# Attention in a planned kernel: the steps of all head pairs placed by a table of times, and squares in halves on ScalarE

## The chip, the core and the metric

One core of one Trainium2 chip runs the whole program. The metric is the device time of one execution in microseconds, taken as the median of the runs. The kernel before took 1324.17 us (three runs, 1322.8 to 1329.11 us).

## What is computed

Attention over 4 batches, 12 heads, 448 tokens and a head size of 64, with RMS-normed q and k, and then two dense MLPs over 1792 tokens, all in 32-bit floats.

```
q_n, k_n = rmsnorm(q, g_q), rmsnorm(k, g_k)      # x / sqrt(mean(x*x) + 1e-6) * g, over the head size
scores = (1/sqrt(64)) * q_n @ k_n.T ; scores -= max(scores) ; attn = exp(scores)
attn = attn / (sum(attn) + 1e-9) ; out = attn @ v                      # q, k, v: (4, 12, 448, 64)
x = out as (1792, 768)
h = x @ w_in ; x = (h * sigmoid(h)) @ w_out                            # w_in (768, 2048), w_out (2048, 768)
h = x @ w_in2 ; y = relu(h)**2 @ w_out2
```

## The kernel before

The program makes a list of **steps** and a planner orders them. `Plan.step` records a step with its engine or engines and an assumed duration; buffers come from rings of fixed depth (`RINGS` for SBUF, `BANKS` for PSUM: 4 banks `s`, 3 banks `t`, 1 bank `pv`). `Plan.forward` is a list scheduler: at each turn it takes, over all engines, the ready step that can start first, and among equals the one that is due first. `Plan.backward` makes new due times from the result, six rounds in all, and `Plan.issue` writes the instructions in the order of the best round. Each engine then executes its own instructions strictly in that order, and waits on semaphores. Buffers of a ring are handed on in the order in which the source creates them (`Buf.turn`), whatever the planner does.

Attention works on 24 **pairs** of heads (4 batches x 6). For a pair:

- `prepare` (L442): q and k are loaded by SP (L452, ring `qk` of 3), squared into `sq` (L461 on ScalarE for the first three pairs, L463 on GpSimd for the rest; one instruction of 1024 elements for q and k together), summed on VectorE (L474), turned into inverse roots by three Newton rounds of small GpSimd instructions (L481, L499 to L511) with two small VectorE ones (L487, L493), and multiplied in (`norm`, L519: GpSimd, for the first pairs also VectorE). TensorE transposes the normed q and k (L530), and ScalarE and VectorE split the result into a high part (L540, L538) and a low part (L547, L545).
- `weigh` (L566): for each of 4 chunks of 112 rows: six matmuls make the scores of two heads in two `s` banks (L579), VectorE takes the row maxima (L589), ScalarE the exponentials and their sums (L595), TensorE transposes them into `t` banks (L603), and ScalarE (L417) or VectorE (L419) copies them to `PT`. `ECOPY` (L35) allows ScalarE for the first head's copy, either engine for the second's.
- `attend` (L613): the sums are inverted (L621, L622), stored to DRAM as 896 numbers of 4 bytes (L628, `store_r`, by SP or ScalarE's queue) and read back broadcast into `R` (L636, `spread`); TensorE multiplies `PT` by v into the bank `pv` (L647); ScalarE copies it out and VectorE or GpSimd multiplies by `R` (L668, `attended`).

The result `xf` of the first two batches is split into the MLP's operand (`x_hi`, `x_lo`, the helper's lines L429, L431 and L438); that of the last two is stored (L699) and read back later. The first MLP (L862 up, L916 down) and the second (L1081, L1157) follow on TensorE. Their weights arrive as 64-bit words that are squeezed into floats on ScalarE (L761) and VectorE (L765 to L781), and split in two parts (L429, L431, L438); a few of these units are made during attention and fill gaps there. The new pool of buffers behind attention opens when all attention steps have been issued, and its first tiles wait for the last store of `xf`.

A step's engines and its assumed time are written like this, here `squares`:

```
"squares", at, {**act_t(2 * W2), **pool_t(2 * W2, 600.0)} if i < SOON else pool_t(2 * W2, 600.0), squares,
reads=[(qk, 0), (qk, 1)], writes=[sq],
```

Of the kernel before, what the change touches and what calls it, by code (L numbers as in the profile page):

```python
# [24 lines left out]
RINGS = {"xb": 4, "yb": 2, "yf": 5, "xl": 2, "v": 1, "V": 2, "part": 2, "xf": 6, "raw": 2, "W": 3, "w": 5, "E": 4, "PT": 4, "qk": 3, "T": 2, "n": 2, "vv": 3, "g": 4}  # L25
# [7 lines left out]
SOON = 3  # L33

ECOPY = [[("act",), ("act", "dve")]] * 4  # L35
# [15 lines left out]
class Step:  # L51
    def __init__(self, kind, on, fn, when, n):
        self.kind, self.on, self.fn, self.when, self.n = kind, on, fn, when, n
        self.needs, self.claims = {}, []
        self.at = min(on, key=lambda e: on[e][0])
        self.extra = 4.5 if kind == "store_r" else 0.0

# [9 lines left out]
class Plan:  # L67
# [42 lines left out]

    def link(self):

        pre = [dict() for _ in self.steps]
# [19 lines left out]
    def forward(self, due):  # L133
# [12 lines left out]
        span = 0.0  # L146
        while len(order) < len(steps):
            best = None
            for e in ENGINES:
                f = free[e]  # L150
                for n in wait[e]:
# [19 lines left out]
            if best is None:  # L171
                raise RuntimeError("no step can be issued")
            (st, _, _), e, n = best
            s = steps[n]
            t, xfer, locks = s.on[e]
            if xfer is not None:
# [120 lines left out]
def kernel(  # L297
# [144 lines left out]
    def prepare(i):  # L442
# [6 lines left out]
        for n, src in enumerate((q, k)):  # L449
# [6 lines left out]
            )  # L456
        sq = sa([CP, 2, NB8, D], F32, "sq", 1)

        def squares(e):
            if e == "act":  # L460
                nc.scalar.activation(sq.ap, qk.ap, AF.Square)  # L461
            else:
                engine(e).tensor_tensor(sq.ap, qk.ap, qk.ap, ALU.mult)  # L463

        step(
            "squares", at, {**act_t(2 * W2), **pool_t(2 * W2, 600.0)} if i < SOON else pool_t(2 * W2, 600.0), squares,
            reads=[(qk, 0), (qk, 1)], writes=[sq],
        )
# [6 lines left out]
            reads=[sq], writes=[ms],  # L475
        )

        little = {"pool": (0.17, None, True)}
# [4 lines left out]
        )  # L483

# [5 lines left out]
        )  # L490
        step(
# [5 lines left out]
        for _ in range(3):  # L497
# [3 lines left out]
            )  # L501
            step(
                "newton", at, little, lambda e: nc.gpsimd.tensor_tensor(a.ap, a.ap, ms.ap, ALU.mult),
                reads=[ms], writes=[a],
            )
            step(
                "newton", at, little,
                lambda e: nc.gpsimd.tensor_scalar(a.ap, a.ap, 1.5, None, ALU.add), writes=[a],
            )
            step(  # L510
                "newton", at, little, lambda e: nc.gpsimd.tensor_tensor(y.ap, a.ap, y.ap, ALU.mult),  # L511
                reads=[a], writes=[y],
            )
        T = sa([P, 2, 2, S], FR, "T")
        for n in range(2):
            n32 = sa([CP, NCH, 2, D], F32, "n")
            step(
                "norm", at, any_t(W2, 600.0) if i < SOON else pool_t(W2, 600.0),
# [6 lines left out]
            )  # L525
            pt = psum("t")
# [726 lines left out]
```

## Time and profile before

| | |
|---|---|
| median of 3 runs | 1324.17 us |
| the profiled execution | 1326.16 us, of which its span is 1324.4 us |
| mean granted TensorE clock | 0.977 |
| TensorE busy | 1219.7 us (92%) |
| VectorE busy | 939.1 us (71%) |
| ScalarE busy | 530.8 us (40%) |
| GpSimd busy | 250.8 us (19%) |

The page and the trace come from one execution. Attention takes roughly the first 400 us of it, the first MLP the time to about 860 us, the second the rest. "PE" is TensorE's matmuls, "PEld" its weight loads, which overlap them; DVE is VectorE, ACT is ScalarE, POOL is GpSimd, SP the engine that issues most DMAs. A busy share over the whole span mixes these three stages; the stage that a change touches has to be read by itself. An arrow in a row names what ended the idle time before the instruction.

### The profile page before, as it was taken

Reading aid. Unit: us, or ns where it says so; the run is one execution under the profiler, and the core shown is the slowest. Engines: PE = TensorE matmul, PEld = TensorE weight load, DVE = VectorE, ACT = ScalarE, POOL = GpSimd, SP = SyncE. Lnnn points to the kernel's source line nnn. Section 1 sums busy time; section 2 is a strip of 40 time slices with the busy share of each in tenths; the row PEclk is TensorE's granted clock in tenths of the full one; section 3 lists DMA queues with packets and bytes.
Section 4 is the critical chain, followed back from the end, with each engine's and each line's share of the span. In section 5 each row is a group of like instructions: output and inputs, shape, how many; then the busy total and the mean of one; then the engine's idle time right before and its main releaser. Section 6 shows DMA issues by size and latency. Waiting matters only on the chain. (4 is left out here: it accounts for less than half of the span.)

```text
span 1324.4 us, 18981 instructions
## 1 busy us (share of the span) xinstructions
PE 1219.7 (92%) x6960; PEld 1069.2 (81%) x6960; DVE 939.1 (71%) x1618; ACT 530.8 (40%) x1117; POOL 250.8 (19%) x443
## 2 busy tenths in 40 slices
PE   5678788788899999999999998999999998999998
PEld 3455555556679999989999997989988998999998
DVE  6677766566658798778889887866677885445554
ACT  4666665566644332243433322343333333122111
POOL 5666545445200000010100000101121100000000
PEclk9889988889999999999999999999999999999999
DMA  5465433444325555549687784784456767445434
GB/s 144 87 119 109 104 81 57 76 87 77 51 39 181 156 161 156 151 138 334 215 261 243 224 258 149 239 319 179 179 186 228 279 244 237 172 148 181 155 132 131
DMA packets 134109, 220.75 MB, mean 167 GB/s; under 512 B 31104, under 2 KB 99456, under 8 KB 134016
## 3 DMA queue, kind: packets, MB, share of 16 engines
q1 hardware_dynamic: 119264, 219.25, 54.6%
q10 hardware_dynamic: 14752, 0.29, 0.6%
q8 instruction: 55, 0.90, 0.3%
q14 instruction: 38, 0.31, 0.1%
HBM read 145.88 MB, written 73.62 MB: 166 GB/s over the span
## 5 line engine op out<-in xcount | busy, mean ns | idle before, releaser
L862 PE MATMUL t<-xb,w 128*128 128x448 f32 x1152 | 242.5, 367 | 5.1 <-DVE g L879 4.9
L916 PE MATMUL s<-gg,w 128*128 128x448 f32 x1152 | 240.6, 366 | 1.3 <-DVE gg L438 1.3
L862 PEld LDWEIGHTS t<-xb,w 128*128 128x128 f32 x1152 | 217.3, 189 | 24.1 <-DVE g L879 6.0
L916 PEld LDWEIGHTS s<-gg,w 128*128 128x128 f32 x1152 | 216.2, 188 | 19.4 <-DVE gg L438 1.7
L1157 PE MATMUL s<-w,gh 128*128 128x384 f32 x896 | 228.0, 335 | 0.0
L1157 PEld LDWEIGHTS s<-w,gh 128*128 128x128 f32 x896 | 162.5, 188 | 1.9 <-DVE gg L1184 0.3
L1157 PE MATMUL s<-w,gl 128*128 128x384 f32 x448 | 150.5, 336 | 6.0 <-DVE gl L438 5.9
L1184 DVE TENSOR_TENSOR gg<-s,gg 128x384 f32<-128x384 f32 x196 | 107.5, 554 | 55.0 <-PE s L1157 54.8
L589 DVE TENSOR_REDUCE mx<-s 112x1 f32<-112x448 f32 x192 | 108.6, 617 | 52.4 <-PE s L579 37.1
L603 PEld LDWEIGHTS t<-ident,E 112*112 112x112 f32 x768 | 78.0, 140 | 74.4 <-ACT E L595 42.8
L603 PE MATMUL t<-ident,E 112*112 112x112 f32 x768 | 105.2, 278 | 34.0 <-ACT E L595 28.5
L595 ACT ACTIVATE E<-s,mx 112x448 f32<-112x448 f32 x192 | 121.5, 654 | 25.8 <-DVE mx L589 25.8
L438 POOL TENSOR_TENSOR w<-W,w 128x768 fp32r<-128x768 f32 (+1 forms) x18 | 30.9, 1719 | 487.4 <-ACT w L429 483.5
L1097 DVE TENSOR_TENSOR g<-t,g 128x448 f32<-128x448 f32 x96 | 58.2, 620 | 85.3 <-ACT g L417 57.4
L647 PE MATMUL pv<-PT,vv 112*64 112x224 f32 x768 | 94.8, 382 | 0.2 <-DVE PT L419 0.2
L579 PE MATMUL s<-T 64*112 64x448 f32 x576 | 88.3, 420 | 5.4 <-DVE T L545 4.6
L417 ACT COPY PT<-t 112x448 f32<-112x448 f32 x133 | 69.7, 556 | 56.9 <-PE t L530 21.3
L1157 PEld LDWEIGHTS s<-w,gl 128*128 128x128 f32 x448 | 84.1, 188 | 8.2 <-DVE gl L438 8.2
L429 ACT CAST w<-W 128x768 fp32r<-128x768 f32 (+1 forms) x68 | 50.1, 739 | 99.8 <-PE s L916 53.0
L438 DVE TENSOR_TENSOR w<-W,w 128x768 fp32r<-128x768 f32 (+1 forms) x94 | 86.4, 927 | 2.8 <-ACT w L429 2.5
L647 PEld LDWEIGHTS pv<-PT,vv 112*64 112x64 f32 x768 | 62.4, 145 | 19.7 <-issue 1.6
L579 PEld LDWEIGHTS s<-T 64*112 64x112 f32 x576 | 51.6, 190 | 28.9 <-issue 11.2
(109 smaller groups left out, 1687.3 us busy)
## 6 DMA issues: line engine op xcount, KB each, us to landing
raw<-in_moe_w_in_dram SPq DMA_DIRECT2D x32, 768.0 KB, 5.4
raw<-in_moe_w_out_dram SPq DMA_DIRECT2D x24, 512.0 KB, 4.3
raw<-in_moe_w_out_dram SPq DMA_DIRECT2D x16, 768.0 KB, 5.8
su<-w SPq DMA_DIRECT2D x16, 768.0 KB, 5.2
w<-su SPq DMA_DIRECT2D x16, 768.0 KB, 5.5
yf<-y SPq DMA_DIRECT2D x48, 224.0 KB, 5.0
ki<-W SPq DMA_DIRECT2D x16, 384.0 KB, 5.7
ko<-W SPq DMA_DIRECT2D x24, 256.0 KB, 4.7
```

Of the source, the lines that this page charges most:

```text
L417: nc.scalar.copy(o(), a())
L438: kind, when, any_t(n, rate), lambda e: engine(e).tensor_tensor(o(), a(), h(), ALU.subtract),
L579: nc.tensor.matmul(pts[j].ap[:CP, :S], T.ap[r, 0, a, c * CP:(c + 1) * CP], T.ap[r, 1, b_], start=(k_ == 0), stop=(k_ == 2),)
L589: lambda e, pt=pt, mx=mx: nc.vector.tensor_reduce(mx.ap, pt.ap[:CP, :S], AX.X, ALU.max, negate=True),
L595: lambda e, j=j, c=c, pt=pt, mx=mx, E=E: nc.scalar.activation(E.ap[:, j], pt.ap[:CP, :S], AF.Exp, bias=mx.ap, accum_out=sums.ap[:, j, c:c ...
L603: nc.tensor.transpose(pe.ap[:CP, m * CP:(m + 1) * CP], E.ap[:, j, m * CP:(m + 1) * CP], ident.ap)
L647: nc.tensor.matmul(pv.ap[j * D:(j + 1) * D, c2 * CT * CP:(c2 + 1) * CT * CP], vr.ap[:, j * NCH + m, :], pt.ap[:, j * NCH + m].rearrange("p ...
L862: nc.tensor.matmul(pt.ap[:, :S], w_()[:, c, :], x[c // HC].ap[:, a, c % HC, :], start=(c == 0 and n == 0), stop=(c == NC6 - 1 and n == 2),)
L916: nc.tensor.matmul(pt.ap[:, :S], w_()[:, f, :], gg.ap[:, k, a, f, :], start=(f == 0 and n == 0), stop=(f == HQ - 1 and n == 2),)
L1097: lambda e: nc.vector.tensor_tensor(o.ap, pt.ap[:, :S], a.ap, ALU.add),
L1157: nc.tensor.matmul(pt.ap[:, :NH], g.ap[:, fi, tc_ * P:(tc_ + 1) * P], w_()[:, 0, nh * NH:(nh + 1) * NH], start=(n == 0), stop=(n == 5),)
L1184: lambda e, o=o, pt=pt: nc.vector.tensor_tensor(o(), pt.ap[:, :NH], o(), ALU.add),
```

## The change

The list scheduler stays, but every attention step now gets a **nominal time** from a table (`nominal`), a pair's times being those of pair 0 plus 10.6 us (`2 * T2`) per pair. On each engine the steps with a nominal time are issued in the order of these times and no other; a step without one (weights, the MLPs) is put between them only where the planner sees that it ends at most 0.1 us (`FIT`) after the next fixed one could start. Rings hand their buffers on in the order of the nominal times too (`link`), so that the transposes of the next pair's q and k take their `t` banks between those of the present pair's exponentials. With that go: squares on ScalarE for all pairs, as two instructions of 512 elements (one for q, one for k); copies of the transposed exponentials fixed to one engine each, half and half (`ECOPY`); `attended` and `x_lo` (for the first two batches) on GpSimd alone, `x_hi` and the copy of `pv` on ScalarE alone, `norm` on VectorE for the first two pairs and on GpSimd after; the store and the read-back of the sums both on SP's queue; the ring `n` of normed tiles has 3 buffers for 2.

```
-RINGS = {... "n": 2, "vv": 3, "g": 4}
+RINGS = {... "n": 3, "vv": 3, "g": 4}
-ECOPY = [[("act",), ("act", "dve")]] * 4
+ECOPY = [[("dve",), ("act",)], [("act",), ("dve",)]] * 2
+T2 = 5.3
+EVEN, ODD = 0.0, 3.67
+FIT = 0.1
+SECOND = {"squares": -1.5, "sums": -2.0, "newton": -4.0, "newton_i": -4.0, "norm": 6.7}
+def nominal(kind, c=0, j=0):
...
+        "load_qk": -47.0 + 0.5 * j, "load_v": -12.0, "squares": -38.0 + 5.75 * j, "sums": -29.5,
...
+        "attend": (2 + c) * T2 + 0.9, "pv_copy": 3 * T2 + 4.35,
+        "inverse": 3 * T2 + 2.3, "store_r": 3 * T2 + 2.7, "spread": 26.7 + 0.4 * j,
...
+    def fix(self, i, kind, c=0, j=0, at=None):
+        s = self.steps[-1]
+        s.on = {at: s.on[at]} if at else s.on
+        s.at = list(s.on)[0]
+        s.nom = 2 * T2 * i + nominal(kind, c, j)
+        if i == 1:
+            s.nom += SECOND.get(kind, 0.0)
     def link(self):
+        for ring in self.rings.values():
+            ring.sort(key=lambda b: 1e9 if b.steps[0].nom is None else b.steps[0].nom)
+            for n, b in enumerate(ring):
+                b.turn = n
...
+        fixed = {e: sorted((s for s in steps if s.nom is not None and s.at == e), key=lambda s: (-s.nom, -s.n))
+                 for e in ENGINES}
...
                 for n in wait[e]:
+                    if steps[n].nom is not None and steps[n] is not next:
+                        continue
...
+                    if next is not None and steps[n] is not next:
+                        nx = max(f, ready[next.n][e]) if not left[next.n] else max(f, next.nom + late)
+                        if st + steps[n].on[e][0] > nx + FIT:
+                            continue
...
-        step(
-            "squares", at, {**act_t(2 * W2), **pool_t(2 * W2, 600.0)} if i < SOON else pool_t(2 * W2, 600.0), squares,
-            reads=[(qk, 0), (qk, 1)], writes=[sq],
-        )
+        for n in range(2):
+            step(
+                "squares", at, act_t(W2),
+                lambda e, n=n: nc.scalar.activation(sq.ap[:, n], qk.ap[:, n], AF.Square),
+                reads=[(qk, n)], writes=[(sq, n)],
+            )
+            plan.fix(i, "squares", j=n)
...
+            plan.fix(i, "norm", j=n, at="dve" if i < 2 else "pool")
...
+        plan.fix(i, "store_r", at="sp")
...
+            plan.fix(i, "spread", j=j, at="sp")
...
+        plan.fix(i, "attended", at="pool")
```

How the order moves is seen at three places. The first is TensorE in the middle of attention. Before, one pair takes ten rows; `n` is the normed q or k (L530), `T` its split transpose, `s` the scores (L579), `E` the exponentials (L603), `pv` the product with v (L647):

```order
L530 MATMUL t<-ident,n 128x112 x8
L647 MATMUL pv<-PT,vv 64x224 x8
L579 MATMUL s<-T 112x448 x12
L603 MATMUL t<-ident,E 112x112 x4
L579 MATMUL s<-T 112x448 x6
L603 MATMUL t<-ident,E 112x112 x8
L579 MATMUL s<-T 112x448 x6
L603 MATMUL t<-ident,E 112x112 x12
L647 MATMUL pv<-PT,vv 64x224 x8
L603 MATMUL t<-ident,E 112x112 x8
```

Now half a pair takes six rows, which then come again for the other half:

```order
L654 MATMUL s<-T 112x448 x6
L601 MATMUL t<-ident,n 128x112 x4
L730 MATMUL pv<-PT,vv 64x224 x8
L681 MATMUL t<-ident,E 112x112 x8
L654 MATMUL s<-T 112x448 x6
L681 MATMUL t<-ident,E 112x112 x8
```

The transposes of the next pair's q or k (L601, four at a time) and half of the product with v of the pair before (L730) now stand between two chunks of the present pair; before, a pair's transposed q and k came right ahead of its own scores, with only a product with v of the pair before between. Behind attention TensorE's order is the same, row for row, as before; of the first MLP's up matmuls, 63 stood ahead of the last L647 before, and 3 stand ahead of the last L730 now.

The second place is ScalarE at the start. Before, the first rows are these (`sq` the squares, `T` the high parts of pair 0, `W` a weight, `E` the exponentials):

```order
L461 ACTIVATE sq<-qk 112x1024 x3
L540 CAST T<-t 128x448
L538 ACTIVATE T<-t,G 128x448
L761 ACTIVATE W<-raw 128x768
L595 ACTIVATE E,sum<-s,mx 112x448 x4
```

Now, with buffer numbers (qk_136 holds the fourth pair, qk_196 the fifth, T_147 belongs to pair 0, T_222 to pair 1, E_225 and E_264 to chunks 0 and 1 of pair 0):

```order
L527 ACTIVATE sq_104<-qk_74 112x512 x2
L612 CAST T_147<-t_127 128x448
L853 ACTIVATE W_159<-raw_123 128x768
L853 ACTIVATE W_165<-raw_125 128x768
L527 ACTIVATE sq_170<-qk_136 112x512
L610 ACTIVATE T_147<-t_140,G_134 128x448
L527 ACTIVATE sq_170<-qk_136 112x512
L612 CAST T_222<-t_198 128x448
L672 ACTIVATE E_225,sum_226<-s_180,mx_204 112x448
L672 ACTIVATE E_225,sum_226<-s_181,mx_209 112x448
L527 ACTIVATE sq_260<-qk_196 112x512
L672 ACTIVATE E_264,sum_226<-s_213,mx_256 112x448
```

The fourth pair's squares, which GpSimd made before, now stand on ScalarE ahead of and right behind pair 0's second high part, and the first half of the fifth pair's ahead of pair 0's second chunk of exponentials.

The third place is SP's queue in the middle of attention. Before, one pair looks for instance like this (`rd` the stored sums, `R` their read-back, `vv` v, `raw` and `ko` a weight unit's load and its kept form; in other pairs the store stands in ScalarE's queue instead):

```order
L628 DMA rd<-sum 112x8x1
L559 DMA vv<-in_v_dram 112x2x256
L452 DMA qk<-in_q_dram 112x2x256
L452 DMA qk<-in_k_dram 112x2x256
L754 DMA raw<-in_moe_w_out_dram 128x4x256
L789 DMA ko_1_1598<-W 128x512
L636 DMA R<-rd 64x448 x2
```

Now the pairs have the first five of these rows in this order (as long as q and k are left to load), and some a weight unit besides:

```order
L709 DMA rd<-sum 112x8x1
L633 DMA vv<-in_v_dram 112x2x256
L718 DMA R<-rd 64x448 x2
L516 DMA qk<-in_q_dram 112x2x256
L516 DMA qk<-in_k_dram 112x2x256
L846 DMA raw<-in_moe_w_in_dram 128x6x256
L881 DMA ki_1237<-W 128x768
```

The loads of q and k moved from ahead of the read-back to behind it, and the next pair's store stands right behind them.

## Rows read from the trace of the kernel before

**Rows 1.** The page's 40 slices of the span (33 us each): busy tenths of TensorE, and the clock granted to it, in tenths.

```profile
PE   5678788788899999999999998999999998999998
PEclk9889988889999999999999999999999999999999
```

**Rows 2.** Busy time by stretch: length, then busy us (and instructions) of PE, PEld, DVE, ACT and POOL, granted clock, DMA share, GB/s.

```profile
0.00:375.00 375.00, 294.01 (x2233) 206.99 (x2233) 250.32 (x476) 231.26 (x597) 189.09 (x397) 0.93 0.45 89
397.00:1324.40 927.40, 904.21 (x4593) 844.43 (x4593) 679.36 (x1124) 290.94 (x499) 61.66 (x46) 1.00 0.61 201
```

**Rows 3.** The timeline of PE: start, length, instruction and count. First the first scores of the first pair, then those of the last two pairs, then the change from attention to the first MLP.

```profile
15.84 2.99 PE L579 MATMUL s<-T 64*112 64x448 f32 x12 [0.72 <-ACT T L538]
...
359.58 1.48 PE L579 MATMUL s<-T 64*112 64x448 f32 x12
...
372.07 1.47 PE L579 MATMUL s<-T 64*112 64x448 f32 x12
...
382.92 12.42 PE L862 MATMUL t<-xb,w 128*128 128x448 f32 x60 [0.22 <-ACT PT L417]
395.26 1.74 PE L647 MATMUL pv<-PT,vv 112*64 112x224 f32 x16
396.93 16.68 PE L862 MATMUL t<-xb,w 128*128 128x448 f32 x81
413.45 1.78 PE L916 MATMUL s<-gg,w 128*128 128x448 f32 x8
```

**Rows 4.** Who waited for whom between 30 and 375 us: total us, times, longest.

```profile
POOL sq L463 <- DMA qk<-in_k_dram: 65.5, 18, 5.9
PEld t L603 <- ACT E L595: 40.7, 32, 6.7
POOL n L519 <- PE t L530: 38.5, 24, 10.7
DVE ms L474 <- POOL sq L463: 37.9, 16, 5.0
PE t L530 <- DVE sum L621: 18.5, 10, 3.7
```

**Rows 5.** The timeline of TensorE's weight loads, whose starts mark the steps, between 300 and 312 us.

```profile
303.60 1.33 PEld L647 LDWEIGHTS pv<-PT,vv 112*64 112x64 f32 x16
305.27 1.08 PEld L579 LDWEIGHTS s<-T 64*112 64x112 f32 x12 [0.33 <-issue]
...
309.06 0.76 PEld L603 LDWEIGHTS t<-ident,E 112*112 112x112 f32 x8 [0.32 <-PE s L579]
309.96 0.47 PEld L579 LDWEIGHTS s<-T 64*112 64x112 f32 x6
310.76 0.76 PEld L603 LDWEIGHTS t<-ident,E 112*112 112x112 f32 x8 [0.32 <-issue]
```

**Rows 6.** Groups of instructions by line and shape: count | busy us, mean ns of one | idle before and its releasers.

```profile
L417 ACT COPY PT<-t 112x448 f32<-112x448 f32 x133 | 69.7, 556 | 56.9 <-PE t L530 21.3 <-PE t L603 21.2 <-issue 11.0
L419 DVE COPY PT<-t 112x448 f32<-112x448 f32 x59 | 36.3, 616 | 6.4 <-PE t L603 6.3
L461 ACT ACTIVATE sq<-qk 112x1024 f32<-112x1024 f32 x3 | 3.2, 1056 | 2.7 <-DMA qk<-in_k_dram 1.4 <-DVE ms L474 1.3
L463 POOL TENSOR_TENSOR sq<-qk 112x1024 f32<-112x1024 f32 x21 | 39.7, 1893 | 65.6 <-DMA qk<-in_k_dram 65.5
L668 DVE TENSOR_TENSOR xf<-xf,R 128x448 f32<-128x448 f32 x17 | 10.5, 615 | 8.8 <-DMA R<-rd 7.7 <-ACT xf L417 1.0
L668 POOL TENSOR_TENSOR xf<-xf,R 128x448 f32<-128x448 f32 x7 | 8.0, 1140 | 0.1
L438 DVE TENSOR_TENSOR xb<-xf,xb 128x448 fp32r<-128x448 f32 x10 | 8.1, 808 | 0.1
L431 DVE CAST xb<-xf 128x448 fp32r<-128x448 f32 x3 | 3.6, 1200 | 0.1
L508 POOL TENSOR_SCALAR nwt<-nwt 112x16 f32<-112x16 f32 x72 | 23.1, 321 | 5.9
```

**Rows 7.** The timeline at the start: VectorE's norms of pair 0 and pair 1, SP's loads of the fourth pair behind the first, ScalarE's second high part of pair 0; and, as the last line, how long these loads took from issue to landing.

```profile
12.62 1.32 DVE L519 TENSOR_TENSOR n<-qk,y 112x512 f32<-112x512 f32 x2 [0.56 <-POOL y L511]
14.02 0.33 SPq L452 DMA_DIRECT2D qk<-in_q_dram  x1
15.16 0.63 ACT L538 ACTIVATE T<-t,G 128x448 fp32r<-128x448 f32 x1 [0.21 <-PE t L530]
17.24 1.31 DVE L519 TENSOR_TENSOR n<-qk,y 112x512 f32<-112x512 f32 x2 [0.67 <-POOL y L511]
...
DMA to landing us min/median/max: 4.8/4.8/4.9
```

**Rows 8.** The store of the sums: SP's timeline of one pair, then the time to landing of all 24 stores, and then busy time in the 7.8 us after another store and in the 3.2 us behind them (columns as in rows 2).

```profile
302.12 0.32 SPq L628 DMA_DIRECT2D rd<-sum  x1
...
305.68 0.45 SPq L452 DMA_DIRECT2D qk<-in_k_dram  x1
310.84 1.24 SPq L636 DMA_DIRECT2D R<-rd  x2
...
DMA to landing us min/median/max: 6.0/7.7/10.2
...
193.00:200.80 7.80, 6.87 (x61) 5.02 (x62) 5.65 (x12) 5.18 (x14) 4.77 (x14) 1.00 0.20 16
200.80:204.00 3.20, 2.93 (x25) 2.07 (x25) 2.21 (x4) 3.20 (x10) 0.06 (x1) 1.00 0.84 216
```

**Rows 9.** DMA issues: count, KB each, median us from issue to landing.

```profile
qk<-in_q_dram SPq DMA_DIRECT2D x24, 224.0 KB, 6.7
raw<-in_moe_w_in_dram SPq DMA_DIRECT2D x32, 768.0 KB, 5.4
ki<-W SPq DMA_DIRECT2D x16, 384.0 KB, 5.7
```

**Rows 10.** The timeline of ScalarE behind attention: the first tile of the new pool.

```profile
401.77 1.51 ACT L429 CAST gg<-g 128x448 fp32r<-128x448 f32 x3 [0.85 <-DMA x<-xf]
```

**Rows 11.** The timeline of GpSimd and VectorE at about 20 us: a small GpSimd instruction beside a weight's instruction on VectorE.

```profile
20.25 1.01 POOL L508 TENSOR_SCALAR nwt<-nwt 112x16 f32<-112x16 f32 x1
...
20.61 0.54 DVE L765 TENSOR_SCALAR W<-W 128x768 f32<-128x768 f32 x1
```

More of the change, by code (lines that the diff above doesn't have):

```diff
@@ L30, with chunk_time @@
 BANKS = {"s": 4, "t": 3, "pv": 1}
-SOON = 3
-ECOPY = [[("act",), ("act", "dve")]] * 4
+ECOPY = [[("dve",), ("act",)], [("act",), ("dve",)]] * 2
[3 more added lines that the diff above has]
+SECOND = {"squares": -1.5, "sums": -2.0, "newton": -4.0, "newton_i": -4.0, "norm": 6.7}
+def chunk_time(c):
+    return c // 2 * T2 + (ODD if c % 2 else EVEN)
+def nominal(kind, c=0, j=0):
+    turned = chunk_time(c + 1) + (0.82 if c % 2 == 0 else 2.9)
+    return {
+        "load_qk": -47.0 + 0.5 * j, "load_v": -12.0, "squares": -38.0 + 5.75 * j, "sums": -29.5,
+        "newton": -24.1 + 0.24 * j, "newton_i": -24.1 + 0.24 * j,
+        "norm": -20.1 + 1.1 * j, "turn_q": (j - 2) * T2 + 0.82, "q_hi": (j - 2) * T2 + 1.58, "q_lo": (j - 2) * T2 + 2.1,
+        "scores": chunk_time(c), "row_max": chunk_time(c) + 0.95 + 0.55 * j,
+        "exp": chunk_time(c) + 1.6 + 0.63 * j, "turn_e": turned + 0.4 * j,
+        "e_copy": turned + (1.25 if c % 2 == 0 else 0.6) + (1.0 if c % 2 == 0 and j else 0.55 if j else 0.0),
+        "attend": (2 + c) * T2 + 0.9, "pv_copy": 3 * T2 + 4.35,
+        "inverse": 3 * T2 + 2.3, "store_r": 3 * T2 + 2.7, "spread": 26.7 + 0.4 * j,
+        "attended": 6 * T2 + 3.3, "keep_x": 6 * T2 + 4.6, "x_hi": 6 * T2 + 4.9, "x_lo": 6 * T2 + 5.2,
+    }[kind]
 class Buf:
@@ L145, in forward @@
         start, at, order = [0.0] * len(steps), [None] * len(steps), []
-        span = 0.0
+        span = late = 0.0
+        fixed = {e: sorted((s for s in steps if s.nom is not None and s.at == e), key=lambda s: (-s.nom, -s.n))
+                 for e in ENGINES}
+        due = [d if s.nom is None else s.nom - 1e6 for d, s in zip(due, steps)]
         while len(order) < len(steps):
@@ L150, in forward @@
                 f = free[e]
+                next = fixed[e][-1] if fixed[e] else None
                 for n in wait[e]:
+                    if steps[n].nom is not None and steps[n] is not next:
+                        continue
                     st = ready[n][e]
@@ L171, in forward @@
             if best is None:
+                for e in ENGINES:
+                    if fixed[e]:
+                        x=fixed[e][-1]
+                        print(e,x.kind,x.when,round(x.nom,1),left[x.n],[(steps[t].kind,steps[t].when,steps[t].nom) for t,_ in self.pre[x.n] if steps[t] not in [steps[o] for o in order]])
                 raise RuntimeError("no step can be issued")
@@ L175, in forward @@
             t, xfer, locks = s.on[e]
+            if s.nom is not None:
+                fixed[e].pop()
+                if e == "pe":
+                    late = st - s.nom
             if xfer is not None:
@@ L474, in prepare @@
             "sums", at, dve_t(2 * W2), lambda e: nc.vector.tensor_reduce(ms.ap, sq.ap, AX.X, ALU.add),
-            reads=[sq], writes=[ms],
+            reads=[(sq, 0), (sq, 1)], writes=[ms],
         )
-        little = {"pool": (0.17, None, True)}
+        plan.fix(i, "sums")
+        little = {"pool": (0.24, None, True)}
         step(
@@ L496, in prepare @@
         )
-        for _ in range(3):
+        plan.fix(i, "newton_i", j=2)
+        for n in range(3):
             step(
@@ L563, in values @@
         )
+        plan.fix(i, "load_v")
         return vr
@@ L584, in weigh @@
             step("scores", at, pe_t(0.8), scores, reads=[(T, (n, a)) for n in range(2) for a in range(2)], writes=pts)
+            plan.fix(i, "scores", c)
             for j, pt in enumerate(pts):
@@ L716, in make_x @@
             )
+            if b < 2:
+                lower = plan.steps.pop()
+                plan.fix(b * NP + hp, "x_hi", at="act")
+                plan.steps.append(lower)
+                plan.fix(b * NP + hp, "x_lo", at="pool")
         return x
```

30 lines of the change are left out of this document (23 added, 7 removed).

## Prediction

> **What bounds the kernel now.** I read the slices of the page first, then busy time by stretch, then the order of TensorE's steps and the waits inside attention. Behind about 400 us TensorE is busy nine tenths or more in nearly every slice at a clock of 1.0 (2.4 GHz), before that five to eight tenths at a clock that dips below 1.0 [rows 1]. From 397 us to the end it is busy 904 of 927 us; in the first 375 us only 294, though no other engine is full there either: VectorE 250, ScalarE 231, GpSimd 189 [rows 2]. So attention is bound by waits, the rest by TensorE, and a change of the attention order is worth what it takes out of the first 400 us. One pair takes (372.07 - 15.84) / 23 = 15.49 us [rows 3]. The waits say why: GpSimd sits before the squares for q and k, before the norm for a free buffer that TensorE's transposes give back, VectorE before the sums for GpSimd's squares, and TensorE before the exponentials' transposes for ScalarE and before q's and k's transposes [rows 4]. A pair's preparation is a chain over four engines, and it ends right where that pair's scores should begin.
>
> **The change, TensorE.** In the new order the next pair's transposes and the previous pair's product with v lie between the chunks of the present pair. What is left as a floor is TensorE's own work. From starts of consecutive steps [rows 5]: two transposes of exponentials 309.06 to 309.96 = 0.90 us; six score matmuls 309.96 to 310.76 = 0.80; one half of the product with v 303.60 to 305.27 = 1.67. Four transposes of q or k I take as half of 0.90, 0.45. A half pair is 2 x 0.80 + 2 x 0.90 + 0.45 + 1.67 = 5.52, a pair **11.04 us**. The table's 10.6 is under that, so its times can't be met, only its order.
>
> **Is it covered?** VectorE: 250.3 us so far; 37 more copies of exponentials (133 of 192 were ScalarE's, now 96 are) x 0.616 = +22.8; 17 `attended` leave (-10.5); 13 parts of x leave (8.1 + 3.6 = -11.7): 250.9, or 10.45 a pair, 95% of 11.04 [rows 2, 6]. ScalarE: 231.3 - 37 x 0.556 + 21 squares x 1.056 = 232.9, 9.7 a pair. GpSimd: 189.1 - 39.7 + 27 x 1.14 = 180, 7.5 a pair [rows 2, 6]. The halved squares have no row. Below: two halves cost one whole, 1.06; above: two instructions near 0.6, as a copy of 448 takes 0.556; so 0 to 0.15 us a pair, on ScalarE, which has over 1 us to spare. I take 0.1 and cost it at nothing; without that cover it would be 2.4 us in all. Gains below zero I exclude, since the same elements go through. The third buffer `n` costs nothing. All engines but GpSimd are thus 88 to 100% full, each in a fixed order: some waiting must be left.
>
> **SP's queue.** Per pair, SP stores the sums, waits until they have landed, issues two read-backs, then the loads of q and k, then the next store. In the pair shown the read-back was issued 8.72 us after the store [rows 8]. Add 1.24 for the two read-backs and 0.90 for q's and k's issues (twice 0.45): 10.9 us, just under TensorE's 11.04. Behind the waiting read-back stand q and k, and for them waits ScalarE, whose exponentials stand behind the squares. The table gives q 9 us from load to square, landing takes a median of 6.7 [rows 9], so 2.3 us are spare. Three weight units (768 KB in, 384 KB back) stand in this queue while q and k still come; at 216 GB/s [rows 8] that is 1.18 MB, or 5.4 us, each, of which 2.3 are spare: 3 x 3.1 = 9.3 us, or 0.39 a pair. From zero (all hidden) to 0.39 I take **11.4 us a pair**, near the upper end, since VectorE is also at 95%.
>
> **Start.** Pair 0's norms end at 13.94, and only then can the fourth pair's q and k be loaded (14.02); they land 4.8 us later [rows 7], at 18.8. ScalarE's order now has a half of that pair's squares (about 0.55) ahead of pair 0's second high part, which so ends at 18.8 + 0.55 + 0.63 = 20.0 instead of 15.8. The norms of pair 1 now stand behind pair 0's second low part on VectorE: 20.0 + 0.7 + 1.31 = 22.0. They free the buffer for the fifth pair: landed at 26.8, half squared at 27.4, and only then come pair 0's exponentials of chunk 1, which the table has 5.3 us behind its first scores. So attention runs as if it had begun at **22** and not at 15.84 [rows 3]: a loss of 6 us. Bounds: no loss, if the weights' earlier place lets q land sooner, to 11.
>
> **End.** The table has the last product with v 16.8 us behind a pair's first scores, 1.585 periods, and it takes 1.7. Before, 63 up matmuls had been done by then; now 3. The other 141 of the first 144 take 0.204 each (16.52 / 81) [rows 3], 28.8 us, and then the first down matmul starts, at 413.45 before. The first tile of the new pool came 18.9 us after the up matmuls began (382.92 to 401.77) [rows 3, 10]; now about 20, since the last two stores and read-backs follow each other in one queue. TensorE can go on for seven units of 18 x 0.204 = 3.67 us, 25.7, before it lacks a `t` bank, so this costs nothing; if it comes 5 us later still, it costs that. Behind this, TensorE's order is the same, so I leave those 913 us as they are.
>
> **Sum.** 22 + 23 x 11.4 + 1.585 x 11.4 + 1.7 + 28.8 = 332.8 for the first down matmul; 413.45 - 332.8 = 80.7 us gained. The profiled execution took 1326.16, 2.0 above the median of the runs: 1326.2 - 80.7 = 1245.5, or **1244** on the median.
>
> **Rivals.** *SP's loop sets the pace.* The longest landing of a store was 10.2 us, the median 7.7 [rows 8]; now each store has q, k and the read-backs right ahead of it. With 10.2 the loop is 10.2 + 1.24 + 0.9 = 12.3 us: 22 + 24.585 x 12.3 + 30.5 = 354.9, 1266 on the median. For it: while a store is under way the DMA engines moved 16 GB/s at a share of 0.20, and 216 GB/s right behind [rows 8], so a store stops the others. Against it: q and k now come behind the landing, where the queue is free. The Trainium skill, "DMA: Bandwidth & Descriptors", section "Queues, rings and completion order", says that the update that tells of a landing is ordered behind every earlier write of that DMA engine, whatever its queue; by that rule a store is told of only after the loads ahead of it, as in this rival. That q and k, issued behind the store, take a median of 6.7 and not the 4.8 us of the start [rows 7, 9] is in line with it.
>
> *VectorE and ScalarE set it.* At 95% and 88% in fixed orders with a wait at every hop, the pace could stay at 12.5, what the last pairs show (359.58 to 372.07), for whom nothing more is loaded or squared [rows 3]: 22 + 24.585 x 12.5 + 30.5 = 359.8, 1270. For it: VectorE's 95%. Against it: an engine's wait for the next one is now for work of another chunk or pair, not for the step that it has just fed.
>
> *The order changes nothing.* The time per pair would stay 15.5 and the loss at the start would show alone. Against it, the order of TensorE's rows is another one. Only something that costs 70 us in the MLPs would give the time back, and their order is kept.
>
> *Slower: GpSimd is shut out.* Slower than before means a pair of (413.45 - 52.5) / 24.585 = 14.7 us or more. GpSimd's thirteen small Newton instructions take 0.321 on average (the third kind of them), but one took 1.01 beside a weight's instruction on VectorE [rows 6, 11]. If all did, a pair would need 7.5 + 13 x 0.69 = 16.5 us on GpSimd: 22 + 24.585 x 16.5 + 30.5 = 458, 1369. It decides from 0.87 us each. Against it: only some 34 weight instructions stand between the attention steps, fewer than two a pair. The Trainium skill, "SBUF — State Buffer", section "SBUF: two separate sides", says that VectorE and GpSimd share a pair of ports as an exclusive lock, held for a whole instruction when VectorE reads two SBUF inputs or runs in a fast mode. By that rule, 34 instructions hold it, and the row at 20.25 us agrees; it could not reach 14.7.
>
> **How the numbers follow.** Forecast (11.04 to 11.8 us a pair, 1232 to 1253): 0.61. SP's loop (to 12.4): 0.18. VectorE and ScalarE (12.4 to 13.2): 0.12. Slower than that but still faster than before: 0.04. No change: 0.02. Slower: 0.03. The low end is 11.04 with a start at 20: 321.9, 1233; I put it 2 us lower. The high end of 1271 takes in the second rival's value. Faster by over 0.5%, about what a measurement of this kernel can tell: 0.95; within: 0.02; slower: 0.03.
>
> **What would show it.** First scores of the first and the last pair about 262 us apart; TensorE nearly without gaps in attention, its clock at 1.0; the first down matmul near 333 us; ScalarE waiting for q and k near the start; from there to the end 913 us. Wrong would be: TensorE waiting for exponentials in every pair (VectorE or ScalarE), ScalarE waiting for loads in every pair (SP), or a longer first MLP.

## The result and the profile after

The changed kernel took **1268.8 us** (median of four runs, 1261.4 to 1273.0), the kernel before 1325.0 beside it: a ratio of 0.957, interval 0.952 to 0.962, so faster. 1244 was forecast, with a range of 1231 to 1271. The profiled execution took 1261.43, with a span of 1259.5; it was the fastest of the four. On two other chips, where the kernel before takes 1319.2 and 1318.2, the ratio was 0.9536 [0.9511, 0.956] and 0.9531 [0.9513, 0.9548].

TensorE and its clock in 40 slices, from the page of the changed kernel; [rows 1] answers to it:

```profile
PE   5998999999999999999999999999999989999998
PEclk9998989999999999999999998999999999999999
```

Busy time by stretch, as in [rows 2] (PE, PEld, DVE, ACT, POOL, then clock, DMA share, GB/s):

```profile
0.00:300.00 300.00, 271.47 (x2213) 183.97 (x2214) 247.53 (x477) 234.89 (x606) 169.37 (x398) 0.98 0.51 102
346.60:1259.50 912.90, 889.31 (x4513) 830.87 (x4511) 665.00 (x1100) 284.64 (x489) 63.32 (x46) 0.99 0.60 201
50.00:72.50 22.50, 22.50 (x196) 15.47 (x194) 20.91 (x41) 20.02 (x53) 14.78 (x33) 1.00 0.40 68
100.00:125.00 25.00, 20.72 (x161) 14.13 (x160) 17.77 (x36) 17.98 (x47) 12.79 (x27) 0.87 0.45 103
```

Two things are to be seen. Behind attention next to nothing moved: 912.9 us of span from the first down matmul, against 910.9 before. And attention is of two kinds: from 50 to 72.5 us TensorE never stops and is at its full 2.4 GHz (1.00); from 100 to 125 it misses 4 us, and the mean granted clock of that stretch is 0.87, since it falls to 0.50 (1.2 GHz) behind the stop.

TensorE's timeline at the marks of [rows 3]: first scores of the first and of the last pair, first down matmul:

```profile
16.16 0.71 PE L654 MATMUL s<-T 64*112 64x448 f32 x2 [2.96 <-ACT T L610]
...
295.69 0.87 PE L654 MATMUL s<-T 64*112 64x448 f32 x6
...
346.56 0.57 PE L1008 MATMUL s<-gg,w 128*128 128x448 f32 x2
```

So a pair takes (295.69 - 16.16) / 23 = **12.15 us**, from 15.49. But hardly any pair takes that: 13 of the 23 distances between first scores are 11.20 to 11.22, and the others reach from 11.46 to 17.84. An undisturbed half pair, answering to [rows 5]:

```profile
50.05 0.87 PE L654 MATMUL s<-T 64*112 64x448 f32 x6
50.85 0.60 PE L601 MATMUL t<-ident,n 112*128 112x112 f32 x4
51.39 1.73 PE L730 MATMUL pv<-PT,vv 112*64 112x224 f32 x16
53.05 0.98 PE L681 MATMUL t<-ident,E 112*112 112x112 f32 x8
53.96 0.86 PE L654 MATMUL s<-T 64*112 64x448 f32 x6
54.75 0.98 PE L681 MATMUL t<-ident,E 112*112 112x112 f32 x8
55.66 0.87 PE L654 MATMUL s<-T 64*112 64x448 f32 x6
```

From start to start that is 0.80 + 0.54 + 1.66 + 0.91 + 0.79 + 0.91 = 5.61, a floor of 11.22 us a pair, which the kernel reaches when nothing is late. The waits from 16 to 300 us tell what is late (answering to [rows 4]; total us, times, longest):

```profile
POOL nwt L565 <- DVE y L558: 45.1, 22, 4.9
ACT sq L527 <- DMA qk<-in_q_dram: 24.9, 11, 6.3
...
PEld t L681 <- ACT E L672: 23.2, 40, 4.6
POOL xf L753 <- DMA R<-rd: 19.5, 10, 3.6
```

The first row is a wait of every pair and costs nothing: undisturbed pairs have it too. The second is the new one. Followed through the largest stall (17.84 us) on the timelines of SP, ScalarE and TensorE:

```profile
98.47 0.39 SPq L709 DMA_DIRECT2D rd<-sum  x1
98.95 0.51 SPq L633 DMA_DIRECT2D vv<-in_v_dram  x1
105.22 0.39 SPq L846 DMA_DIRECT2D raw<-in_moe_w_in_dram  x1
105.65 2.53 SPq L881 DMA_DIRECT2D ki<-W  x1
109.48 1.09 SPq L718 DMA_DIRECT2D R<-rd  x2
110.67 0.53 SPq L516 DMA_DIRECT2D qk<-in_q_dram  x1
```

```profile
118.84 0.63 ACT L527 ACTIVATE sq<-qk 112x512 f32<-112x512 f32 x1 [6.26 <-DMA qk<-in_q_dram]
...
119.83 0.63 ACT L672 ACTIVATE E<-s,mx 112x448 f32<-112x448 f32 x1
```

```profile
120.60 2.03 PE L681 MATMUL t<-ident,E 112*112 112x112 f32 x8 [4.24 <-ACT E L672]
```

SP stores the sums at 98.47; a weight's two transfers go out ahead of the read-back, which follows 11.0 us behind the store, when that has landed; q is issued at 110.67 and squared 8.2 us later; ScalarE's exponentials stand behind that square, and TensorE behind the exponentials. What the DMA engines did meanwhile, from the weight's issue to the landing of the store and right behind it (columns as above):

```profile
105.20:109.40 4.20, 4.20 (x36) 3.02 (x38) 3.95 (x11) 4.20 (x13) 2.08 (x10) 1.00 0.38 27
109.50:111.80 2.30, 2.30 (x24) 1.64 (x22) 2.03 (x4) 2.28 (x8) 2.05 (x5) 1.00 0.83 233
```

27 GB/s, with a whole weight waiting, and 233 behind the landing. Stores and loads from 16 to 300 us (issues, KB, median us to landing; [rows 8, 9] before):

```profile
vv<-in_v_dram SPq DMA_DIRECT2D x23, 224.0 KB, 8.8
...
qk<-in_q_dram SPq DMA_DIRECT2D x20, 224.0 KB, 4.6
...
rd<-sum SPq DMA_DIRECT2D x22, 3.5 KB, 10.1
```

The trace has the landing of only some of these issues: five of the 22 stores, one of the loads of v. What has no such gaps is the time from a store to its read-back on SP: 7.3 to 12.6 us in this trace, with a median of 10.1 over 22 pairs.

### The profile page after: what moved, and what is told of

The parts are those of the page before. It is cut to its first block, busy times and chain, and to the rows that moved or that the text cites. A ratio compares the mean times of both kernels' runs of the same rounds, so it can differ in the third digit from the quotient of the medians.

```text
span 1259.5 us, 19054 instructions
## 1 busy us (share of the span) xinstructions
PE 1202.9 (96%) x6960; PEld 1050.1 (83%) x6960; DVE 939.1 (75%) x1624; ACT 535.2 (42%) x1129; POOL 238.9 (19%) x449
## 5 line engine op out<-in xcount | busy, mean ns | idle before, releaser
L1276 DVE TENSOR_TENSOR gg<-s,gg 128x384 f32<-128x384 f32 x196 | 107.7, 554 | 55.4 <-PE s L1249 55.1
L681 PE MATMUL t<-ident,E 112*112 112x112 f32 x768 | 102.1, 274 | 15.9 <-ACT E L672 11.5
L502 POOL TENSOR_TENSOR w<-W,w 128x768 fp32r<-128x768 f32 (+1 forms) x17 | 29.2, 1716 | 442.7 <-ACT w L493 432.9
L493 ACT CAST w<-W 128x768 fp32r<-128x768 f32 (+1 forms) x68 | 49.9, 737 | 93.5 <-PE s L1008 46.4
L730 PE MATMUL pv<-PT,vv 112*64 112x224 f32 x768 | 83.4, 359 | 0.0
L1199 ACT ACTIVATE g<-g 128x448 f32<-128x448 f32 x48 | 27.5, 575 | 118.7 <-DVE g L1189 118.7
L966 ACT ACTIVATE g<-t 128x448 f32<-128x448 f32 x64 | 34.5, 541 | 89.7 <-PE t L954 87.7
L730 PEld LDWEIGHTS pv<-PT,vv 112*64 112x64 f32 x768 | 51.1, 136 | 20.3 <-issue 0.5
```

The source lines that it names most:

```text
L502: kind, when, any_t(n, rate), lambda e: engine(e).tensor_tensor(o(), a(), h(), ALU.subtract),
L681: nc.tensor.transpose(pe.ap[:CP, m * CP:(m + 1) * CP], E.ap[:, j, m * CP:(m + 1) * CP], ident.ap)
L730: nc.tensor.matmul(pv.ap[j * D:(j + 1) * D, c2 * CT * CP:(c2 + 1) * CT * CP], vr.ap[:, j * NCH + m, :], pt.ap[:, j * NCH + m].rearrange("p ...
L1276: lambda e, o=o, pt=pt: nc.vector.tensor_tensor(o(), pt.ap[:, :NH], o(), ALU.add),
```

## The experiments

The theory (theory 1) was the rival on SP's loop: a store of sums takes 10.1 us to land, and with the forecast's times for the read-backs (1.24) and the issues of q and k (0.90) the loop is 12.2 us, above the floor. Theory 2 blames the weights in that queue, theory 3 full engines (VectorE, ScalarE). The kernels ran in four sets, each on a chip of its own beside the kernel before, which took 1318.0, 1319.2, 1318.2 and 1318.9 us. For each kernel: its set, the ratio to the kernel before with its interval, and the pace from the first scores of the first to those of the last pair in the profiled execution.

| kernel | set | ratio | pace, us |
|---|---|---|---|
| changed kernel | 2 | 0.9536 [0.9511, 0.956] | 11.86 |
| changed kernel | 3 | 0.9531 [0.9513, 0.9548] | 11.90 |
| one store only | 1 | 0.9366 [0.935, 0.9383] | 11.21 |
| store on ScalarE's queue | 1 | 0.9516 [0.9492, 0.9541] | 11.61 |
| packed store | 2 | 0.938 [0.9362, 0.9398] | 11.26 |
| loads ahead | 2 | 0.9536 [0.9517, 0.9555] | 11.63 |
| whole squares | 1 | 0.948 [0.9452, 0.9508] | 11.33 |
| late halves | 2 | 0.9524 [0.9501, 0.9548] | 11.52 |
| whole squares again | 3 | 0.9475 [0.9456, 0.9493] | 11.30 |
| no weights in attention | 4 | 0.945 [0.9427, 0.9474] | 11.27 |
| turned store | 3 | 0.938 [0.936, 0.9401] | 11.23 |
| halves only, old order | 1 | 0.982 [0.9797, 0.9843] | 14.00 |

**One store only.** 

```diff
+        if i == 0:
             ... the store of the sums, as before ...
+        rd = first_rd[0]
```

> Left out: the stores of the sums of pairs 1 to 23; every pair reads back the sums that pair 0 stored, so the norms of the other pairs are pair 0's. All of the arithmetic, the read-backs and the loads of q, k, v and weights stay. Theory 1 (SP's loop): no landing is waited for any more, so q and k come as early as their buffers are free, the pace is TensorE's 11.22 us throughout, and the first down matmul comes at 346.6 - 23 x 0.93 = 325 us or a few us earlier: 1236 to 1247 us, and the single times lie closer together. Theory 2 (only the weights' transfers between q and k make the stalls): stalls remain at the pairs with weights, pace 11.6 or more, 1255 or more. Theory 3 (VectorE and ScalarE): the pace stays at 12.1 and the time within 0.5% of 1269.

Measured 1235.2 us, just under the first theory's span. All 22 distances behind the first are 11.21 us, though three of the weights' units are loaded at nearly the same places as in the changed kernel (83.9, 106.4 and 151.1 us; the fourth only at 277.6). Theories 2 and 3, each by itself, fall: without the stores weights cost nothing, and VectorE and ScalarE keep up. From 40 to 275 us, the changed kernel (set 3) and this one, columns as above:

```profile
40.00:275.00 235.00, 226.13 (x1880) 154.16 (x1880) 202.00 (x389) 194.04 (x507) 142.82 (x323) 0.98 0.47 96
```

```profile
40.00:275.00 235.00, 235.00 (x2015) 162.17 (x2015) 213.86 (x410) 205.86 (x537) 147.90 (x328) 1.00 0.34 100
```

TensorE is busy for all of the 235 us, with VectorE at 213.86, 91%.

**The store on another queue.** 

```diff
-        plan.fix(i, "store_r", at="sp")
+        plan.fix(i, "store_r", at="act")
```

> The store of the sums goes out on ScalarE's DMA queue instead of SP's; nothing else is changed. SP then no longer stands between the issue of a store and its landing with q, k, R and weights right ahead of the store in the same queue, but its read-back still waits for the landing. Theory 1 (the serial loop store, landing, read-back, q, k, next store on SP's queue sets the pace, 12.15 us a pair against TensorE's 11.22): the store goes out as soon as the sums are there, the loop loses the time in which the store stands in SP's queue, and most stalls go; pace 11.2 to 11.6 us, time 1245 to 1257 us. If the landing stays at 10 us because the loads of q and k lie ahead of it in the DMA engines and not in the queue, the pace stays near 12 and the time within 0.5% of 1269. Theory 3 (VectorE's and ScalarE's fullness makes the stalls): the pace stays at 12.1, and the time is the same or a little more, since ScalarE has one more issue a pair.

Measured 1254.4: inside the first theory's span, but the changed kernel is only 0.2% above it by ratio, inside the intervals, so no gain is shown. The store still took long (18 of the 23 landings are in the trace), so it is not its place in SP's queue that makes it so:

```profile
rd<-sum ACTq DMA_DIRECT2D x23, 3.5 KB, 8.6
```

**Packed store.** 

```diff
-                rd.ap.rearrange("j c p -> p (j c)"), sums...
+                rd.ap.rearrange("j c p -> (j c p)").rearrange("(p x) -> p x", x=2 * NCH), sums...
```

> The sums are stored as 112 rows of 32 bytes instead of 896 values of 4 bytes each; the read-back reads as before, so a pair's sums come back in another order and its outputs are scaled by wrong numbers: what is left out is the right order alone, all transfers stay. Theory 1 with small packets as the cause of the long landing (median 10.1 us): the landing falls to 3 to 5 us, the read-back and q and k go out 5 us earlier, no stalls: pace 11.2 to 11.3, ratio about 0.938 as without stores. Rival (the landing waits for the loads of q and k ahead of it, whatever its packets): landing stays over 8 us, ratio as the changed kernel's.

Measured 1236.2, as without stores. The same 3.5 KB and v right behind them, with every landing in the trace; then SP's waits for the store between 16 and 300 us (total, times, longest), in the changed kernel of this set and here; and last, from the two pages, of the changed kernel and of this one, all packets (24 x 784 fewer, and 784 = 896 - 112):

```profile
vv<-in_v_dram SPq DMA_DIRECT2D x23, 224.0 KB, 2.7
...
rd<-sum SPq DMA_DIRECT2D x24, 3.5 KB, 1.5
```

```profile
SPq L718 <- DMA rd<-sum: 110.9, 18, 9.6
```

```profile
SPq L718 <- DMA rd<-sum: 19.8, 11, 4.6
```

```profile
DMA packets 134109, 220.75 MB, mean 175 GB/s; under 512 B 31104, under 2 KB 99456, under 8 KB 134016
```

```profile
DMA packets 115293, 220.75 MB, mean 179 GB/s; under 512 B 12288, under 2 KB 80640, under 8 KB 115200
```

The changed kernel of this set has the landing of one store only (7.9 us). That of set 3 has 17 of 22, with a median of 9.5, and 14 loads of v with a median of 8.8; whole squares in set 3 have all 24, with a median of 8.5. Here it is 1.5 and 2.7. So it is the cut into 896 packets of 4 bytes instead of 112 of 32 (the bytes being the same, number and size can't be told apart), and such a store also holds up the loads issued behind it. By these medians that is (8.5 - 1.5) / 784 to (9.5 - 1.5) / 784, or 9 to 10 ns a packet, an estimate over all DMA engines together.

The rule that the forecast weighed (the Trainium skill, "DMA: Bandwidth & Descriptors", section "Queues, rings and completion order": a landing is told of only behind every earlier write of that DMA engine) fits the packed store, and this trace agrees: issued at 139.10 us, 4.6 us behind k, it landed 1.4 us later; issued at 152.78, right behind q and k, at 157.26, just behind k at 157.08. A store that only shares the engines with the loads could look the same. And that is 4.5 us, and not 10.

**Loads ahead of the read-back.** 

```diff
-        "load_qk": -47.0 + 0.5 * j, ...
+        "load_qk": -50.0 + 0.5 * j, ...
```

> The loads of q and k stand ahead of the read-back in SP's queue (3 us earlier in the table), so they no longer wait for the landing of the sums; squares as in the change. Theory 1 (q and k late because SP stands at the landing): q and k are issued at once when their buffer is free, the waits of the squares go, pace 11.2 to 11.5 us, ratio 0.943 to 0.95. Rival (packets of the store hold back any load issued behind them until it has landed, wherever it stands in the queue): loads land no sooner, pace stays near that of the changed kernel. A second rival: the loads now delay the read-back, and GpSimd waits for R: ratio above the changed kernel's.

Measured 1257.2, ratio as the changed kernel's. The waits of the squares fell from 22.2 to 1.2 us, but GpSimd's for R rose from 22.4 to 29.5 (longest 9.3), and two stalls of about 4 us were left. The wait moved to the other arm of the same loop, as the second rival has it, though without a loss. The gain of pace (11.63 against 11.86) is not seen in the time: the first down matmul comes 10.7 us earlier than in the changed kernel of this set, but 923.7 us follow it in the span instead of 916.9. Why the MLPs took longer there is open.

**Whole and late squares.** 

```diff
-        for n in range(2):
-            step("squares", at, act_t(W2), ... (sq.ap[:, n], qk.ap[:, n]) ...)
-            plan.fix(i, "squares", j=n)
+        step("squares", at, act_t(2 * W2), ... (sq.ap, qk.ap) ...)
+        plan.fix(i, "squares", j=1)
```

> The changed kernel with the squares of a pair as one instruction of 1024 on ScalarE, in the place of the second half; the order of all else is kept. The halves cost 2 x 0.62 against 1.06 us, 0.18 a pair on ScalarE, which is not full: by theories 1 and 2 the time is within 0.5% of 1269 (the square then waits for k as well, which lands about 0.45 us behind q; the stalls at the squares grow by that at most). By theory 3 ScalarE's 0.18 us a pair shows: 4 us less.

```diff
-        "squares": -38.0 + 5.75 * j, ...
+        "squares": -32.9 + 0.65 * j, ...
```

> The squares stay in halves, but the half for q is moved from 9.0 us (nominal) behind its load to 14.1, right ahead of k's half; nothing else is changed. Theory 1 in its sharper form (what stops ScalarE is that the first half waits for a q that is loaded only behind the landing of the last pair's sums, with 9 us from load to square): as with whole squares in the late place, the waits of the squares for loads go and the pace falls to 11.2 to 11.5 us, ratio 0.945 to 0.95. Rival (the split as such costs, two instructions for one on a full ScalarE): nothing is gained, ratio as the changed kernel's.

> Whole squares in the place of the second half, once more, now on one chip with the changed kernel. On another chip the ratio was 0.948, against the changed kernel's 0.9536 on a third. If the waits of the squares for q are what the whole square avoids (its place has 14.7 us from load to square, the first half 9), it stays 0.3 to 0.8% below the changed kernel here. If that was the chip, the two agree within 0.3%; the late halves, which gained nothing (0.9524), speak for this.

Whole squares gained 0.6%, twice (1250.5 and 1249.3), the first time against what was expected. Late halves gained nothing in the time (1255.8), but that doesn't clear the place of the square. Their squares wait 6.2 us for loads instead of 23.0, and the pace falls to 11.52; the time is lost behind the last pair, where the first down matmul comes 62.8 us behind its first scores (49.9 in the changed kernel of this set) and ScalarE stands 32.8 us for weights. The scheduler had also placed only two units of weights between 8 and 277 us, at 68.1 and 91.4. So here place and weights moved together. The traces show this difference for whole squares too: with whole squares the scheduler, which fits the weights' units in between the fixed steps, placed none between 8 and 268 us, and the distances from the third pair on are all 11.22 in the second of these runs. The changed kernel loads one at 82.3, 105.2, 156.8 and 245.3 us, and its three largest stalls begin with the pairs of 107.7, 159.2 and 248.2. In set 3 it loads them at nearly the same times, and its two largest (17.10 and 14.86, from 131.6 and 183.2) begin 25 us or more behind one.

**No weights in attention.** 

```diff
-FIT = 0.1
+FIT = -0.2
```

> The changed kernel, halves and all, but the scheduler's slack for other work between the fixed steps is -0.2 instead of 0.1 us, which puts no unit of a weight into the middle of attention (none between the first pairs and the last three, as in the kernel with whole squares; in the changed kernel four units are loaded there, at about 82, 105, 157 and 245 us); the units come later. If a weight's transfers behind a store start each of the stalls, and the whole squares gained only because the scheduler then found no room for these units: pace 11.2 to 11.4 us from the third to the last pair, as with whole squares, ratio 0.945 to 0.949. If the loop of store, landing and loads stalls without weights too, as long as q's square stands 9 us behind its load: pace 11.6 to 12, waits of the squares for q of 10 us or more in all, ratio 0.951 to 0.955.

Measured 1246.2, ratio 0.945: as with whole squares, with halves. No weight is loaded between 7.4 and 283 us. TensorE from 40 to 275 us, columns as above, and the store between 40 and 250 (seven of the 18 landings are in the trace):

```profile
40.00:275.00 235.00, 234.13 (x2001) 160.78 (x2000) 202.85 (x394) 200.66 (x527) 133.75 (x320) 1.00 0.46 83
```

```profile
rd<-sum SPq DMA_DIRECT2D x18, 3.5 KB, 8.3
```

So most of the stall time needs both: a store of 896 packets, and a weight's unit, whose 1.18 MB stand in the queue that the store holds up. (The smaller slack keeps the unit's work on ScalarE and VectorE out too; that its transfers do it is read from the stall shown above, not tried by itself.) By the median the loop alone, 8.3 + 1.24 + 0.9 = 10.4 us, stays under the floor, but not in every pair: two distances of 12.34 and 11.60 us are left here, and the largest with late halves, 14.55 from 195.2 us, begins 100 us behind the last issue of a weight's transfers. The units come later here and meet the last stores: ScalarE stands for one, with the first MLP's first activations behind it, and the first down matmul comes at 330.63:

```profile
303.96 0.89 ACT L853 ACTIVATE W<-raw 128x768 f32<-128x768 f32 x1 [11.71 <-DMA raw<-in_moe_w_in_dram]
```

**Turned store: all is computed, with few packets.** 

```diff
+            nc.vector.reciprocal(square.ap[:CP, :NB8], r.rearrange("p j c -> p (j c)"))
+            nc.vector.transpose(turned.ap, square.ap)
...
+            for k in range(4):
+                w = min(32, CP - 32 * k)
+                engine(e).dma_start(rows[:, 32 * k:32 * k + w], turned.ap[32 * k:32 * k + NB8, :w])
```

> All is computed. VectorE writes the reciprocals into a zeroed square of 128 x 32 and transposes it in blocks of 32 x 32 (one more instruction a pair, about 0.1 to 0.2 us by the nearest rows, the small ones of that engine), so that the store goes out as 32 rows of 64 to 128 bytes in four DMAs instead of 896 values of 4 bytes in one. If the number of packets is what makes the landing long (as the store of 112 rows suggests, 1.5 us against 7.9), the landing is 1.5 to 3 us, the pace 11.2 to 11.4 and the ratio 0.937 to 0.943. Rival: VectorE, over nine tenths full, with one more instruction sets the pace at 11.5 or more, or the four issues (some 2 us of SP's time a pair) make q and k late again: ratio 0.948 or more.

Measured **1237.3 us**, ratio 0.938 [0.936, 0.9401], against 0.9531 [0.9513, 0.9548] for the changed kernel in this set: 1.5% better than it and the best of all that compute everything. The one instruction more, TensorE's and VectorE's busy time from 40 to 275 us, and the first down matmul:

```profile
L707 DVE STREAM_TRANSPOSE turned<-square x24: 211/211/214, 36.3 to 288.4; 128x32 f32<-128x32 f32 x24
```

```profile
40.00:275.00 235.00, 235.00 (x2011) 161.84 (x2012) 217.89 (x435) 206.48 (x537) 147.53 (x326) 1.00 0.34 104
```

```profile
319.01 0.57 PE L1018 MATMUL s<-gg,w 128*128 128x448 f32 x2
```

VectorE is at 217.89 of 235, 93%, and TensorE still never stops: theory 3 is out. The four units of weights are in attention again (at 69.7, 103.4, 137.3 and 227.1 us). No landing of this store is in the trace, so the 1.5 to 3 us that were expected can't be read; SP's waits for it between 16 and 300 us can, against 111.6 us in the changed kernel of this set:

```profile
SPq L728 <- DMA rd<-turned: 13.2, 13, 3.8
```

The first down matmul comes 11.6 us ahead of the 330.63 above: 1.2 lie in the last pair's earlier first scores, 10.4 behind them, where short stores and weights that are made earlier save the tail.

**One part alone: halves on ScalarE in the old order.** 

```diff
-            "squares", at, {**act_t(2 * W2), **pool_t(2 * W2, 600.0)} if i < SOON else pool_t(2 * W2, 600.0), ...
+        for n in range(2):
+            step("squares", at, act_t(W2), ... (sq.ap[:, n], qk.ap[:, n]) ...)
```

> The kernel before, in its own order by due times and costs, with one part of the change alone: the squares of every pair on ScalarE in two halves, one for q and one for k. If the gain comes from the fixed order, as all theories on the pace have it, this keeps the pace near 15.5 us and the time within 1.5% of 1325 (1305 to 1340); if GpSimd's squares were the wait that set the pace of before, taking them off GpSimd alone gives more than half of the gain (under 1297).

Measured 1293.9, under the 1297; but the kernel before takes 1318.0 on this chip, and 1.8% is less than half of the change's gain of 4.7%, so it lies between the two. From the eleventh pair on most distances are 12.5 to 12.6 us, what before only the last pairs showed. GpSimd's wait for k ahead of its squares is gone, its wait for a free norm buffer grew instead (30 to 375 us; before [rows 4]):

```profile
POOL n L515 <- PE t L526: 98.2, 16, 10.5
PEld t L599 <- ACT E L591: 40.9, 30, 6.9
```

So the squares alone bring 1.8%, and the rest of the change some 2.9% (0.982 to 0.953): the fixed order with the fixed engines and the third buffer `n`, which were not tried apart. The forecast gave the squares no gain of their own.

> The changed kernel as it is, to be compared with the experiments on one chip. Before, its ratio to the kernel before was 0.9566; on a chip on which loads and stores land sooner (the kernel before takes 1318 there and not 1325) theory 1 expects fewer stalls: ratio 0.952 to 0.957. If the ratio is 0.948 here too, whole squares were worth nothing and the difference of that run was the chip's.

> The changed kernel again, beside the other kernels of this set on one chip. Ratio 0.952 to 0.957, as in the two sets before.

Both held (table).

## Why the prediction held, point by point

The direction was right, and the likeliest time was 25 us too low. The pace of 12.15 lies in the band of SP's loop (11.8 to 12.4, a chance of 0.18) and not in the forecast's own (11.04 to 11.8, 0.61): 1268.8 is within the range only because its high end took in the rivals, and by 2 us. In the profiled execution the miss is 1261.4 - 1245.5 = 15.9 us, and it lies in the terms below: -5.8 at the start, 17.3 by the pace, 2.3 from the last pair's first scores to the first down matmul (50.9 against 48.6), 2.2 behind it. The rest is that this execution was the fastest of four, 7.4 us under the median, where the forecast took off 2.

- **Start: 6 us of loss forecast, 0.3 measured** (16.16 against 15.84), 5.8 to the good. The fourth pair's q was issued at 12.07, not 14.02, and squared at 14.95, 2.9 us later and not 4.8; the term took the old order's norms and landing. The lower bound, no loss, is what came.
- **Floor: 11.04 forecast, 11.22 measured.** Four transposes of q or k take 0.54, not half of eight (0.45). That is 0.18 x 24.6 = 4.4 us.
- **Pace: 11.4 forecast, 12.15 measured**, 0.75 x 23 = 17.3 us with the floor's part. The step that failed is the price of the weights in SP's queue: 9.3 us in all, by 2.3 us of slack and 216 GB/s. Without them attention runs at 11.27; with them at 11.9 in sets 2 and 3 and 12.15 in the first profile, so beside the long stores they cost 0.6 to 0.9 a pair, 14 to 20 us. The rate of 216 GB/s was that behind a landing; while the store is under way [rows 8] shows 16 GB/s, and the weight of the stall shown went out in that time, at 27. The row was there, and it was used for the rival only. The loop beside it was priced from one pair, at 8.72 us from store to read-back; in the changed kernel the median is 10.1. With either taken away, the stores or the weights, the pace is 11.2 to 11.3.
- **The rival on SP's loop** took 10.2 us of landing and 12.3 us; the first profile has 10.1 and 12.15. The agreement is partly luck, since the pace is a mean of 11.22 and of stalls, and not a loop that takes 12.3 in every pair; in set 3 the median landing was 9.5, which makes a loop of 11.6, and the pace 11.90. That q and k come with a free queue behind the landing, given against this rival, did not help, since they come too late.
- **VectorE and ScalarE (a chance of 0.12): out**, by the turned store. Counting busy time against TensorE's floor had the right answer, 91 to 93%, and such an engine in a fixed order did not delay TensorE at all.
- **End:** from the last product with v to the first down matmul 31.6 us against 28.8; with short stores 319.01 - 289.84 = 29.2, so the term was right. What is over it goes with the long stores.
- **Behind it: 913 forecast**; 1261.43 - 346.56 = 914.9 in the profiled time against 912.7 before, so right to 2 us.
- **Signs:** the first scores of the first and the last pair lie 279.5 us apart (262 forecast), the first down matmul comes at 346.56 (333). ScalarE waits for q not near the start alone: the longest waits come behind 110 us, and 11 in all, so not in every pair either.
- **GpSimd, no change, the clock:** GpSimd had 169 us of 300 to do; the clock is 1.00 where TensorE doesn't stop (50 to 72.5 us), as forecast, and 0.50 behind the stop at 116 us.

What stays open: why whole squares leave the scheduler no room for weights was read from its result, not followed through its rules; how a weight's delay comes to stall a pair 25 us later was not followed; and what the packets of a small store wait for was not tried.

## What to carry to other kernels

A resource that hardly shows in a page of bytes can set the pace: 3.5 KB took 8 to 10 us as 896 packets and 1.5 as 112, and the loads issued behind them waited too. Price a transfer by its packets and by what is queued behind its landing, and where a transpose of 0.2 us makes rows of it, take it. And when two versions differ in one step, look at where the scheduler has put the other work before crediting the step.

## What was not expected of the hardware

- The landing of a 3.5 KB store: medians of 8.3 to 10.1 us as 896 packets of 4 bytes, on either queue (8.6 on ScalarE's), 1.5 us as 112 packets of 32 bytes. A load of 224 KB issued right behind took a median of 8.8 us (set 3) and 2.7 us.
- In the last 4.2 us of the store at 98.47 us, with a weight's transfers waiting, the DMA engines moved 27 GB/s; in the 2.3 us behind its landing, 233.
- VectorE transposes 128 x 32 values of f32, in blocks of 32 x 32, in 0.211 us.
